# An attention and MoE kernel whose written order of steps is made anew, with seven more warm-up products

## The chip, the cores and the metric

The kernel runs on 1 core of one Trainium2 chip. The metric is the device time of one execution in microseconds (us), the median of several runs. PE (TensorE) multiplies matrices into PSUM, which is made of eight banks; DVE (VectorE) and ACT (ScalarE) read PSUM and write the on-chip memory; POOL (GpSimd) works on the on-chip memory alone; SP (SyncE) issues most of the transfers.

## The reference

```python
def _attn_ref(x, state):          # x 8x8x512x64, state 8x8x32x64
    scores = scale * np.matmul(x, state.transpose(0, 1, 3, 2))
    ...
    xread = np.matmul(a, state)              # a = softmax(scores)
    scores2 = scale * np.matmul(state, x.transpose(0, 1, 3, 2))
    ...
    sread = np.matmul(a2, x)                 # a2 = softmax(scores2)
    return np.concatenate([xread, sread], axis=2)

def _moe_ref(x, g_ln, w_ch1, w_ch2):         # x 8x544x512 from the attention
    xn = (x - mu) / np.sqrt(var + 1e-06) * g_ln
    ch = np.maximum(xn @ w_ch1, 0.0) @ w_ch2
    return x + ch
```

For each of 8 batches there are two small softmax attentions between x (512 rows, 8 heads) and state (32 rows). Their results, 544 rows of 512 numbers, go through a layer norm and a two-layer perceptron of 512, 2048 and 512 numbers, and are added to it. Everything is float32; the kernel keeps that precision by splitting each number into two float16 halves (hi and lo) and adding three products.

## The kernel before, in words

**Units.** The hidden layer's 2048 numbers are taken in four parts, u = 0 to 3. For each batch, a matrix for each part (`state_products`, tile `matrix`) folds state and the first weights together, so the first layer is a product of `matrix` with the attention's numerators `ea`. Batch 0 goes by simple loops while the weights are still being read and split. Batches 1 to 7 go by `products(b)`: two halves g of the rows, four parts u, so 56 units. Four more units (`products(B)`, first stage on L839) do the 32 state rows of all batches.

**One unit.** PE makes two banks `half` on L829, 12 products each (`block(1)`, then `block(0)`). Every one is read by both ACT and DVE. Of `block(1)`, ACT copies a part into `rs` and a part into `xs` (the hi half), and DVE makes a difference in `rs` and the lo half in `xs`. Of `block(0)`, ACT copies hi into `xs`, and DVE makes three sums in `rs` and the lo half. Then ACT and POOL turn the sums in `rs` into hi and lo halves in `xs` (`strassen_hidden`). With these, PE makes 42 products on L887 into four banks `acc`, by Strassen's scheme (`strassen_products`, four steps of 18, 6, 12 and 6 products, with the weights `w2h` and their prepared sums `sums`). After four units `together` adds the banks up in `strip` and `xr` and stores them. The pool of `half` has two banks and the pool of `banks` one pair, so PE can fill one again only when all its readers are done.

**Attention.** While the units of one batch run, the attention of the next is made between them: load of x in two pieces (`x_f`) and of state, split (`x16`) and transposing transfers, scores (L430) in `banks`, the softmax steps on DVE, ACT and POOL (`ts`, `mA`, `mB`, `dA`, `eB`, `eb`, `ef`, `ea`, most of them 128 x 1024 elements), a read of the state (L507). Then eight transfers copy `ea` to `ek`, one copies the upper part of `ek` from the lower, and the product on L537 (`mix`) reads `ek`.

**What sets the order.** All steps are recorded as streams of closures. `issue` calls them in the order that the table `PLAN` gives: an item `67:62` is step 62 of stream 67. Each engine runs its instructions in that order; between engines the program waits by semaphores, which the recording layer places from the order and from what each step reads and writes. It also orders any two reads of one PSUM bank by two engines: the one that is written later waits for the other. The products of `warmth`, `WARM` of them, multiply ones into a bank that nobody reads; the plan puts them where PE has nothing to do in the first 40 us.

```python
def issue(tc, streams, plan):
    streams = [list(s) for s in streams]
    with tc.manual_schedule():
        for item in plan.split() or [f"{k}:0-{len(s)}" for k, s in enumerate(streams)]:
            k, n = item.split(":")
            n = [int(v) for v in n.split("-")]
            for f in streams[int(k)][n[0]:n[-1] + 1]:
                f()
```

Of the kernel before, what the change touches and what calls it, by code (L numbers as in the profile page):

```python
# [165 lines left out]
)  # L166
WARM = 112


class Later:  # L170
# [832 lines left out]
```

## Time and profile before

| | |
|---|---|
| median of 3 runs | 682.26 us (679.79 to 683.41) |
| the profiled execution, its own time | 682.87 us |
| its span, first to last instruction | 680.8 us |
| mean granted clock of PE | 0.995 |
| read from HBM, written | 28.05 MB, 9.44 MB |
| busy share: PE, DVE, ACT, POOL | 94%, 73%, 54%, 33% |

The page gives for each engine the time in which it worked and, in forty slices of the span, how much of each was work. A row of the waits says which engine and line stood, which engine and tile it waited for, and how long in total, how often and at most. A row of the timeline gives start, length, engine, line, operation, tile written and tiles read, sizes and count, and in brackets how long the engine stood idle before it and who ended that. Matmuls are pipelined: two rows that follow each other overlap in the records. Most steps are recorded on L192, the helper `do`, so they are told apart by their tiles.

### The profile page before, as it was taken

How to read it: one execution, taken by the hardware profiler on the slowest of the kernel's cores; microseconds unless marked ns; L12 is line 12 of the kernel's file. 1: busy time of each engine (PE TensorE's matmuls, PEld its weight loads, DVE VectorE, ACT ScalarE, POOL GpSimd, SP SyncE). 2: the span in 40 equal slices, each digit the busy share in tenths (PEclk: the TensorE clock that was granted, in tenths of full speed). 3: DMA queues.
4: the chain of work that ended last, by engine and by line, in shares of the span. 5: the costliest groups of instructions: out<-in, count | busy, mean ns of one | idle time of the engine just before them, and what ended most of it. 6: DMA issues, size and time to landing. Idle time of an engine off the chain costs nothing. (4 is left out here: it accounts for less than half of the span.)

```text
span 680.8 us, 15966 instructions
## 1 busy us (share of the span) xinstructions
PE 643.0 (94%) x6640; PEld 501.3 (74%) x6640; DVE 495.1 (73%) x990; ACT 367.0 (54%) x659; POOL 225.1 (33%) x189
## 2 busy tenths in 40 slices
PE   9999999999999998999999999988999999999995
PEld 3455655768778786778777878776878777888885
DVE  3999996767668688677867796678568786665443
ACT  4589976755454654475546554655276434353341
POOL 0015224411335324413623363145323451333231
PEclk9999999999999999999999999999999999999999
DMA  8976766330032533404250416052311225011002
GB/s 312 279 258 253 204 115 141 64 111 5 19 59 55 150 68 101 112 34 87 55 140 32 104 27 161 23 99 65 82 37 30 43 40 151 32 34 24 9 1 93
DMA packets 90039, 63.15 MB, mean 93 GB/s; under 512 B 69296, under 2 KB 82096, under 8 KB 89520
## 3 DMA queue, kind: packets, MB, share of 16 engines
q1 hardware_dynamic: 87696, 58.18, 32.4%
q0 software_dynamic: 864, 3.15, 2.4%
q8 instruction: 52, 0.85, 0.5%
q10 hardware_dynamic: 1408, 0.82, 0.4%
q14 instruction: 19, 0.16, 0.1%
HBM read 28.05 MB, written 9.44 MB: 55 GB/s over the span
## 5 line engine op out<-in xcount | busy, mean ns | idle before, releaser
L887 PEld LDWEIGHTS <-xs 128*128 128x128 f16 x2520 | 243.7, 98 | 40.8 <-issue 7.9
L192 POOL TENSOR_TENSOR xs<-rs,xs 128x512 f16<-128x512 f32 x120 | 143.3, 1202 | 282.8 <-ACT xs L192 196.4
L887 PE MATMUL acc<-w2h,xs 128*128 128x256 f16 x1440 | 182.7, 274 | 0.0
L829 PE MATMUL half<-ea,matrix 128*128 128x256 f16 x1344 | 163.1, 274 | 14.1 <-DVE rs L192 5.9
L829 PEld LDWEIGHTS <-matrix 128*128 128x128 f16 x1344 | 128.8, 98 | 39.2 <-DVE xs L192 8.4
L887 PE MATMUL acc<-sums,xs 128*128 128x256 f16 x1080 | 143.7, 273 | 2.9 <-DVE strip L192 1.6
L192 DVE SCALAR_TENSOR_TENSOR rs<-half,rs 128x256 f32<-128x256 f32 x224 | 90.6, 417 | 48.9 <-ACT rs L192 21.2
L192 ACT ACTIVATE xs<-rs 128x512 f16<-128x512 f32 (+1 forms) x128 | 77.6, 618 | 67.6 <-DVE rs L192 61.2
L192 ACT ACTIVATE xs<-half 128x256 f16<-128x256 f32 (+1 forms) x112 | 54.1, 486 | 71.5 <-DVE rs L192 41.8
L192 DVE SCALAR_TENSOR_TENSOR xs<-half,xs 128x256 f16<-128x256 f32 (+1 forms) x112 | 60.9, 548 | 24.9 <-ACT xs L192 22.0
L192 ACT ACTIVATE rs<-half 128x256 f32<-128x256 f32 x56 | 21.2, 379 | 48.5 <-PE half L829 37.9
L192 DVE SCALAR_TENSOR_TENSOR matrix<-banks,hs,matrix 128x1024 f16<-128x1024 f32 x28 | 35.8, 1279 | 15.6 <-ACT matrix L192 15.6
L745 PE MATMUL acc<-w2h,hid 128*128 128x512 f16 x192 | 43.4, 379 | 0.3 <-POOL hid L192 0.3
L192 DVE TENSOR_TENSOR strip<-acc,strip 128x256 f32<-128x256 f32 (+1 forms) x60 | 32.9, 548 | 10.6 <-PE acc L887 6.5
L192 ACT ACTIVATE matrix<-banks,hs 128x1024 f16<-128x1024 f32 x28 | 31.1, 1111 | 15.3 <-PE banks L690 14.4
L745 PEld LDWEIGHTS <-hid 128*128 128x128 f16 x192 | 18.2, 98 | 21.4 <-POOL hid L192 0.8
L192 POOL TENSOR_TENSOR hid<-strip,hid 128x512 f16<-128x512 f32 x16 | 20.4, 1285 | 27.9 <-ACT hid L192 25.8
L192 POOL TENSOR_TENSOR ts<-ts,mA 128x1024 f32<-128x1024 f32 (+1 forms) x8 | 16.2, 2022 | 39.3 <-DVE of_weights L192 28.3
L192 PE MATMUL half<-ones 128*128 128x512 bf16 x112 | 27.8, 401 | 1.1 <-DVE ones L322 1.1
L192 DVE SCALAR_TENSOR_TENSOR xr<-strip,of_second,xr 128x512 f32<-128x512 f32 x28 | 26.1, 933 | 2.8 <-POOL strip L192 2.7
L192 ACT ACTIVATE x<-x_f,x_s 128x512 f16<-128x512 f32 x32 | 21.7, 715 | 11.0 <-DVE x_s L192 11.0
L192 DVE SCALAR_TENSOR_TENSOR x<-x_f,x_s,x 128x512 f16<-128x512 f32 x32 | 24.9, 799 | 3.7 <-ACT x L192 3.2
(149 smaller groups left out, 785.0 us busy)
## 6 DMA issues: line engine op xcount, KB each, us to landing
raw<-in_moe_w_ch_dram SPq DMA_DIRECT2D x10, 1024.0 KB, 8.4
out_dram<-xr SPq DMA_DIRECT2D x16, 512.0 KB, 3.3
x_f<-in_x_dram SPq DMA_DIRECT2D x15, 512.0 KB, 5.1
sums<-in_moe_w_ch_dram SPq DMA_DIRECT2D x6, 1024.0 KB, 7.6
ek<-ea SPq DMA_DIRECT2D x56, 64.0 KB, 2.0
ek<-ek SPq DMA_DIRECT2D x7, 512.0 KB, 4.3
xr<-part POOLq DMA_DIRECT2D x6, 512.0 KB, 4.9
s_r<-in_state_dram SPq DMA_DIRECT2D x28, 64.0 KB, 3.5
```

Source lines behind the costliest of these rows:

```text
L192: return lambda: f(*map(now, args), **{k: now(v) for k, v in kw.items()})
L745: nc.tensor.matmul(po, lhsT=hid[:, i, q, c * P:(c + 1) * P], rhs=w[:, j, q], start=first and q == 0 and n == 0, stop=last and q == 3 and n ...
L829: nc.tensor.matmul(ps[:, 256 * q:256 * q + 256], lhsT=m[:, h, i, P * (2 * k + q):P * (2 * k + q) + P], rhs=ea[:, 0, j, h, 256 * g:256 * g ...
L887: nc.tensor.matmul(po[o], lhsT=y[:, n, i, o] if o < 2 else x[:, o - 2, n, i], rhs=v[j], start=u == 0 and n == 0 and k == 0 and o in (2, 1, ...
```

## The change

`PLAN` is written anew as a whole, and `WARM` goes from 112 to 119. Nothing else differs: the same 2554 steps of the streams beside the warm-up, with the same sizes, buffers and operations, are called in another order. One line of the table on each side:

```diff
-    "176:12 176:8 176:11 176:10 176:13-16 "
+    "176:1-2 176:4-5 175:3 176:3 157:9 176:6-7 166:8 176:9-11 176:8 176:12 176:15 176:14 176:16 176:13 "
...
-WARM = 112
+WARM = 119
```

One line shorter, every line number behind the table is less by one: L829 before is L828 after, and L192 is L191.

Two places. The first is DVE in the softmax of batch 6, while units of batch 5 run. `half_6618` and `half_6702` before, `half_6584` and `half_6641` after, are the two banks of one unit; mA, mB, dA and eb are softmax steps. Before:

```order
L192 SCALAR_TENSOR_TENSOR rs_6647<-half_6618,rs_6647 128x256
L192 TENSOR_SCALAR mB_6644<-mB_6644,es_6398 128x2
L192 TENSOR_REDUCE dA_6693<-ts_6632 128x32
L192 SCALAR_TENSOR_TENSOR xs_6690<-half_6618,xs_6690 128x2x128
L192 TENSOR_SCALAR dA_6693<-dA_6693 128x32
L192 TENSOR_SCALAR rs_6716<-mv_6251 128x4
L192 RECIPROCAL dA_6693<-dA_6693 128x32
L192 SCALAR_TENSOR_TENSOR eb_6700<-eB_6697,eb_6700 128x1024
L192 SCALAR_TENSOR_TENSOR rs_6647<-half_6702,rs_6647 128x256
L192 SCALAR_TENSOR_TENSOR xs_6690<-half_6702,xs_6690 128x2x256
L192 SCALAR_TENSOR_TENSOR rs_6647<-half_6702,rs_6647 128x256 x2
```

And after, on the same engine for the same unit:

```order
L191 SCALAR_TENSOR_TENSOR rs_6658<-half_6584,rs_6658 128x256
L191 STREAM_TRANSPOSE ts_6686<-banks_6620 128x1024
L191 TENSOR_REDUCE mA_6688<-ts_6686 128x32
L191 SCALAR_TENSOR_TENSOR rs_6658<-half_6641,rs_6658 128x256
L191 TENSOR_REDUCE mB_6706<-banks_6620 128x2
L191 SCALAR_TENSOR_TENSOR rs_6658<-half_6641,rs_6658 128x256
L191 SCALAR_TENSOR_TENSOR xs_6690<-half_6641,xs_6690 128x2x256
L191 TENSOR_SCALAR mB_6706<-mB_6706,es_6654 128x2
L191 SCALAR_TENSOR_TENSOR xs_6690<-half_6584,xs_6690 128x2x128
L191 TENSOR_REDUCE dA_6744<-ts_6686 128x32
L191 TENSOR_SCALAR dA_6744<-dA_6744 128x32
L191 SCALAR_TENSOR_TENSOR rs_6658<-half_6641,rs_6658 128x256
```

The first read of the second bank moved from behind dA and eb to ahead of mB and dA; eb now comes behind all reads of both banks.

The second place is SP around the copies of `ek` for batch 3. Before:

```order
L192 DMA ek_3841<-ea_3754 32x2x512 x8
L192 DMA sread_rows_104<-sread_3864 32x128
L192 DMA s_r_3982<-in_state_dram 32x8x64
L192 DMA sread_rows_104<-sread_3864 32x128
L192 DMA ek_3841<-ek_3841 64x4096
L192 DMA s_r_3982<-in_state_dram 32x8x64 x3
```

And after:

```order
L191 DMA ek_3758<-ea_3737 32x2x512 x8
L191 DMA ek_3758<-ek_3758 64x4096
L191 DMA sread_rows_104<-sread_3961 32x128
L191 DMA x_f_4013<-in_x_dram 128x4x256
L191 DMA sread_rows_104<-sread_3961 32x128
```

The large copy now follows the eight small ones directly; behind it stand a small store and then a 512 KB load of x_f, where three loads of state stood.

243 rows, old and new, of the table PLAN are left out of this document.

## The prediction

> **What bounds the kernel now.** I read the page first, then what PE waited for, then the timeline around the longest of those waits.
>
> ```profile
> span 680.8 us, 15966 instructions
> PE 643.0 (94%) x6640; PEld 501.3 (74%) x6640; DVE 495.1 (73%) x990; ACT 367.0 (54%) x659; POOL 225.1 (33%) x189
> ...
> PE   9999999999999998999999999988999999999995
> ...
> DVE  3999996767668688677867796678568786665443
> ...
> PEclk9999999999999999999999999999999999999999
> ```
>
> PE is busy in every slice, at the full granted clock, and no other engine comes near it. The work is the same before and after, so only three things can change: the time in which PE stands, the warm-up products that fill its first 40 us, and the tail behind its last product.
>
> ```profile
> 672.22 1.47 PE L887 MATMUL acc<-w2h,xs 128*128 128x256 f16 x12
> ...
> 675.90 1.74 SPq L192 DMA_DIRECT2D out_dram<-xs  x4
> ```
>
> PE ends at 672.22 + 1.47 = 673.7 us and was busy for 643.0, so it stood for **30.7 us**. The tail is 680.8 - 673.7 = 7.1 us. This is what PE stood for (us in total, times, longest):
>
> ```profile
> PE half L829 <- DVE rs L192: 5.9, 4, 2.8
> PE half L829 <- DVE xs L192: 5.6, 7, 1.7
> PE banks L537 <- DMA ek<-ek: 4.5, 3, 2.0
> PE half L829 <- DVE of_second L192: 1.6, 1, 1.6
> PE acc L887 <- DVE strip L192: 1.6, 2, 1.1
> PE banks L690 <- DVE matrix L192: 1.2, 1, 1.2
> PE half L192 <- DVE ones L322: 1.1, 1, 1.1
> ...
> PE acc L639 <- DVE raw L192: 1.0, 1, 1.0
> PE banks L537 <- PE acc L777: 1.0, 1, 1.0
> ...
> PE half L829 <- ACT xs L192: 0.7, 2, 0.4
> ...
> PE acc L639 <- DVE sums L192: 0.5, 1, 0.5
> ```
>
> Rows on `half` at L829 are PE waiting for a bank whose old content ACT and DVE haven't yet read: 5.9 + 5.6 + 1.6 + 0.7 = **13.8 us**. Rows on L537 are the product that needs the loaded tile ek: 4.5, and 1.0 for batch 1, which I count with it (the row names PE, but that product needs ek too): **5.5 us**. The other 30.7 - 13.8 - 5.5 = 11.4 us are scattered, 2.6 of them in the first 40 us (the rows of ones, raw and sums).
>
> **Reads of one bank.** One of the longest waits, and the largest one:
>
> ```profile
> 548.35 0.60 ACT L192 ACTIVATE xs<-half 128x512 f16<-128x512 f32 x1 [4.97 <-DVE rs L192]
> 549.03 1.16 PE L829 MATMUL half<-ea,matrix 128*128 128x256 f16 x9 [1.67 <-DVE xs L192]
> ...
> 470.76 2.56 DVE L192 SCALAR_TENSOR_TENSOR eb<-eB,eb 128x1024 f16<-128x1024 f32 x1 [0.58 <-ACT eb L192]
> 473.24 0.41 DVE L192 SCALAR_TENSOR_TENSOR rs<-half,rs 128x256 f32<-128x256 f32 x1
> 473.69 0.60 ACT L192 ACTIVATE xs<-half 128x512 f16<-128x512 f32 x1 [2.47 <-DVE rs L192]
> 474.92 0.75 DVE L192 SCALAR_TENSOR_TENSOR rs<-half,rs 128x256 f32<-128x256 f32 x2
> 475.73 1.59 PE L829 MATMUL half<-ea,matrix 128*128 128x256 f16 x9 [2.83 <-DVE rs L192]
> ```
>
> ACT's copy of `half` into xs uses nothing that DVE's rs makes, yet it stood for 4.97 and 2.47 us until that rs had been read out of the same bank: the program makes the second reader of a bank wait for the first, in the written order. DVE's rs was late itself, queued behind the wide eb, and PE waited at the end of it for 1.67 and 2.83 us.
>
> The new order moves this. In each of the 56 units two banks are read by both engines, 112 in all. Counted in the two orders (each sequence of readers by engine, leaving out changes of engine where the second needs the first's data), the reader changes engine 116 times before and 94 times now; ACT follows DVE with no other step written between 15 times before and 2 times now. At the 2.83 us place the first DVE read of the second bank now stands ahead of mB and of dA, and far ahead of eb. So the change does what it says there.
>
> How much of 13.8 us goes? If it went with all changes of engine, 94 of 116 would be left and the saving is 13.8 x 22/116 = 2.6; if with the closest ones, 2 of 15 are left and it is 12.0. Below nothing it can go too (the last rival). The 2.47 us wait is of the close kind and the 4.97 us one is DVE's own queue, so I take the middle, **-6.9**.
>
> At that place there is a second cause. The same eb took 1.37 us at another place, and 2.56 here, with a POOL operation beside it:
>
> ```profile
> 472.19 2.00 POOL L192 TENSOR_TENSOR rs<-rs,mhalf 128x4 f32<-128x4 f32 x1
> ...
> 543.77 1.37 DVE L192 SCALAR_TENSOR_TENSOR eb<-eB,eb 128x1024 f16<-128x1024 f32 x1
> ```
>
> That is 1.2 of the 2.83 us which no order of bank reads removes. The Trainium skill, SBUF — State Buffer, "Who interferes with whom", speaks against the change here: a DVE instruction with two SBUF inputs shares a read interface with GpSimd, and one of them blocks. By that page the loss lies in DVE and POOL meeting, and the bank term would shrink towards nothing; the 2.56 against 1.37 us agrees with it at this one place.
>
> **Loads.**
>
> ```profile
> ek<-ek SPq DMA_DIRECT2D x7, 512.0 KB, 4.3
> ...
> 283.93 0.52 SPq L192 DMA_DIRECT2D ek<-ek  x1
> ...
> 289.95 0.91 PE L537 MATMUL banks<-sk,ek 128*128 128x64 f16 x16 [1.95 <-DMA ek<-ek]
> ...
> 497.76 0.77 PE banks L690 x24
> ...
> 526.13 1.31 PE half L829 x12
> 527.44 1.97 PE acc L887 x18
> ```
>
> ek is copied in two steps, eight small transfers and then the large one, 4.3 us in the median and here 289.95 - 283.93 = 6.0. What hides it is the PE work written between the step that makes ea's second half (DVE) and the product. By the last three rows, 1.31 / 12 = 0.109 us a product, this cover was 9.6 us for batch 3 and is 13.3 now, and 8.1 and now 12.1 for batch 4; for batch 2 it falls from 16.0 to 13.9. On SP the large copy now follows the small ones directly, where two small stores and a load stood between; what follows it is a 512 KB load of x_f, no longer three small ones, which may slow it. The added cover of 3.7 and 4.0 us is over the longest wait, 2.0. The saving lies between 0 (the loads in flight grow by as much) and 5.5; I take **-4.5**, leaving one wait of 1.0 for batch 2.
>
> The Trainium skill, DMA: Bandwidth & Descriptors, "Anatomy of one DMA", gives about 2.0 us and 436 KB a us for a DMA, which makes an estimate of 3.2 us for 512 KB; by that the cover was enough already and nothing is gained. The 4.3 and 6.0 us here disagree, and the measured waits decide.
>
> **Warm-up.**
>
> ```profile
> 11.71 5.35 PE L192 MATMUL half<-ones 128*128 128x512 bf16 x24
> ...
> 39.12 3.07 PE L639 MATMUL acc<-raw,gm 128*128 128x512 f32 x6 [1.01 <-DVE raw L192]
> ...
> 20.00:40.00 20.00, 18.07 (x146) 8.55 (x145) 18.62 (x35) 12.80 (x15) 1.05 (x1) 1.00 0.78 254
> 80.00:100.00 20.00, 19.85 (x144) 10.23 (x142) 19.62 (x39) 14.96 (x19) 5.18 (x5) 1.00 0.66 140
> ```
>
> Seven products of 5.35 / 24 = 0.22 us are added: 1.5 us on PE. They lie in front of products that waited for DVE (0.5 and 1.0 us in the waits above), in a stretch where DVE (third pair in the windows) is busy for 18.6 and later 19.6 of 20 us. If DVE sets the time they cost 0, if PE does, 1.5. I take **+0.7**.
>
> **The rest.** The last 42 products, the DVE steps after them and the stores stand in the same order; the tail stays at 7.1. The products of the last unit start 5.9 us of PE work behind the last first-stage product, where 9.2 lay before; the steps between (on ACT and DVE one copy of 0.6, three reads of 0.4, another copy of 0.6 and a subtraction of 0.7) make some 3.2, so it stays covered. The other 11.4 us of waits are places that the new order moves as well, and nothing says where to: 0, with -4 to +4 as its bounds, a third of them each way.
>
> **Sum:** -6.9 - 4.5 + 0.7 = -10.7 us. The profiled execution took 682.87 us, 2.1 around its span of 680.8, and lies 0.6 above the median, 682.26. From the median: 682.3 - 10.7 = 671.6, so **672**.
>
> **Rivals.**
> - **Loads alone.** The waits on `half` are DVE's queue and its meetings with POOL, not reads of banks (for it: 4.97 us in a queue and 2.56 us for eb; against: the close crossings fall from 15 to 2). 682.3 - 4.5 + 0.7 = 678.5. Chance 0.17, two thirds of it within 0.5%.
> - **More goes.** All of 13.8 and 5.5 and 4 of the rest: 682.3 - 13.8 - 5.5 - 4 + 0.7 = 659.7. For it: nearly all the closest crossings go, and the loads' cover grows by more than their waits. Against: at 24 places (32 before) ACT still follows DVE with no PE work written between. Chance 0.13 for 666 or less.
> - **Nothing changes**, the order differs and the waits move: 682. Chance 0.04.
> - **Slower: wide steps between reads of one bank.** Between the first and the last DVE read of a bank there stands at least one DVE step of 1.1 us or more at 30 banks (27 before), and two or more at 13 (7 before). Each holds the bank from PE, as eb did. It decides where they and the reads last longer than the PE work until the bank's next use, which is 4 us or less at 16 banks now, 15 before. Six more such places at 1.9 us (the mean of the four longest waits on `half`: 2.83, 1.67, the 1.6 of its third row, and 1.42 below) are 11.4: 682.3 - 4.5 + 0.7 + 11.4 = 690. Against it: 85 banks free of wide steps before and 82 now is nearly the same. Chance 0.14.
>
> ```profile
> 204.30 0.94 PE L829 MATMUL half<-ea,matrix 128*128 128x256 f16 x7 [1.42 <-DVE rs L192]
> ```
>
>
> **How the numbers follow.** The forecast (667 to 677) has 0.52. The range of 662 to 685 leaves out half of "more goes" and most of "slower". A difference under 0.5% (3.4 us) is what a measurement here can't tell from no change. Faster: 0.52 + 0.13 + a third of 0.17 = 0.71; the same: 0.11 + 0.04 = 0.15; slower 0.14.
>
> **What would show it.** In the changed profile, PE busy is about 644.5 and its idle time before its last product some 18 to 20 us; the L537 row on ek is under 1.5; the rows of `half` on DVE and ACT together are 5 to 9, and the 2.83 us wait in the softmax of the last batch but one is gone. If the `half` rows stay near 13 with long DVE steps before them, "loads alone" or "slower" was right; if the L639 and L690 waits vanish and the product of L507 still comes 1.5 us later, the warm-up was paid in full.

## The result, and the profile after

| | before | after |
|---|---|---|
| median, us | 681.31 (679.79 to 683.41, 4 runs) | 662.80 (662.01 to 663.94, 4 runs) |
| the profiled execution | 682.87 | 663.94 |
| its span | 680.8 | 662.1 |

The ratio is 0.9728, with a 95% interval of 0.9694 to 0.9761: 18.5 us less, where the forecast had 10.7 less. The page of the changed kernel, its first lines, and from its timeline PE's last products and the last stores:

```profile
span 662.1 us, 15974 instructions
PE 641.5 (97%) x6647; PEld 502.0 (76%) x6647; DVE 496.2 (75%) x990; ACT 368.3 (56%) x659; POOL 220.6 (33%) x189
...
653.89 1.47 PE L886 MATMUL acc<-w2h,xs 128*128 128x256 f16 x12
...
657.57 1.74 SPq L191 DMA_DIRECT2D out_dram<-xs  x4
```

PE ends at 653.89 + 1.47 = 655.4 and stood for 13.9 us before that, where it was 30.7. The tail is 6.7 us (7.1). DVE does the same work in about the same time (496.2 us, 495.1 before). What PE waited for now, the rows that the text uses:

```profile
PE half L828 <- DVE xs L191: 2.5, 3, 1.2
...
PE half L828 <- DVE rs L191: 1.0, 3, 0.5
PE banks L536 <- issue: 1.0, 1, 1.0
...
PE half L828 <- DVE matrix L191: 0.7, 2, 0.4
```

The rows on `half` at L828 are 2.5 + 1.0 + 0.7 = 4.2 us (13.8 before). The row on L536 is 1.0 (5.5); it names no releaser, but it lies in batch 4, whose large copy took 6.3 us and landed 0.1 us before the product began. All others together 13.9 - 4.2 - 1.0 = 8.7 (11.4). So of the 18.6 us of span, waits on `half` gave 9.6, loads 4.5, other waits 2.7. The warm-up products cost 1.6 more, by their groups in the two profiles:

```profile
L192 PE MATMUL half<-ones 128*128 128x512 bf16 x112 | 27.8, 401 | 1.1 <-DVE ones L322 1.1
```

```profile
L191 PE MATMUL half<-ones 128*128 128x512 bf16 x119 | 29.4, 399 | 1.1 <-DVE ones L321 1.1
```

PE's other products show 643.0 - 27.8 = 615.2 us before and 641.5 - 29.4 = 612.1 now, 3.1 less for the same instructions; the tail gave 0.3. An estimate covers most of the 3.1: a product's record is 0.273 us long and adds 0.109 where the next one overlaps it, so each gap between PE's records costs 0.164 us of busy time; there are 50 gaps before and 35 now, which makes 15 x 0.164 = 2.5. The sum is -9.6 - 4.5 - 2.7 + 1.6 - 3.1 - 0.3 = -18.6.

The place of the prediction's 2.83 us wait, in the timeline of the changed kernel:

```profile
461.02 2.08 DVE L191 SCALAR_TENSOR_TENSOR eb<-eB,eb 128x1024 f16<-128x1024 f32 x1
...
461.98 2.00 POOL L191 TENSOR_TENSOR rs<-rs,mhalf 128x4 f32<-128x4 f32 x1
...
465.35 0.83 PE L886 MATMUL acc<-w2h,xs 128*128 128x256 f16 x6 [0.37 <-DVE xs L191]
```

eb is slow here too, 2.08 us with a POOL step beside it. But PE has 38 products of L886 to work on from 460.66 to 464.97 us, and stands for only 0.37 us behind them.

**Five stretches.** One table explains more than the waits do. Each row below is the stretch from the scores of a batch (L430, L429 after) to the product that reads ek (L537, L536), for batches 2 to 6 (batch 1 overlaps the front, and batch 7's L537 comes 59 us behind its scores): the stretch in us from the span's start, its length, PE's busy time in it. Before:

```profile
195.20:227.80 32.60, 29.41 (x358) 1.00 0.27 59
256.30:290.00 33.70, 28.35 (x329) 1.00 0.41 97
323.10:351.90 28.80, 26.47 (x300) 1.00 0.36 78
390.90:420.10 29.20, 27.80 (x310) 1.00 0.30 63
460.60:493.30 32.70, 29.87 (x317) 0.95 0.32 71
sum 157.00, PE 141.89; mean PE 28.38
```

And after:

```profile
196.10:224.30 28.20, 27.73 (x348) 1.00 0.33 74
249.60:280.50 30.90, 29.32 (x340) 1.00 0.27 58
318.40:349.30 30.90, 29.20 (x340) 1.00 0.36 88
386.40:420.30 33.90, 33.41 (x394) 1.00 0.43 97
449.80:479.80 30.00, 29.18 (x341) 1.00 0.42 104
sum 153.90, PE 148.84; mean PE 29.77
```

The five stretches together are about as long as before, 153.9 and 157.0 us, and PE stands in them for 5.1 us in place of 15.1. That is 10.0 of the 16.8 us of idle time that went. PE's work in them grew by 7.0 us, but the sums hide where. In batches 2, 3 and 6 PE stood for 3.2, 5.4 and 2.8 us, and now for 0.5, 1.6 and 0.8: 8.5 of the 10.0. Its work there is no larger (87.6 us before, 86.2 now); these three stretches got shorter, from 99.0 to 89.1 us. The added work lies in batches 4 and 5 (54.3 and 62.6 us), where PE had stood for only 3.7 us. (In batch 6 before, PE's granted clock was 0.95, and its work there is somewhat inflated by that.) Before, the product that ends a stretch begins within 0.2 us of the landing of ek in all five, so the chain sets their length; now it begins 0.1 to 1.4 us behind it.

DVE's second step on ea, from which the transfers to ek follow, shows where the stretches got shorter. Batch 2 before, and after:

```profile
196.27 1.22 DVE L192 TENSOR_REDUCE mB<-banks 128x2 f32<-128x1024 f32 x1 [1.56 <-PE banks L430]
...
200.53 1.25 DVE L192 STREAM_TRANSPOSE ts<-banks 128x1024 f32<-128x1024 f32 x1 [2.19 <-ACT eB L192]
...
215.13 1.21 DVE L192 SCALAR_TENSOR_TENSOR ea<-ef,ea 128x1024 f16<-128x1024 f32 x1
```

```profile
197.16 1.25 DVE L191 STREAM_TRANSPOSE ts<-banks 128x1024 f32<-128x1024 f32 x1
...
201.49 1.22 DVE L191 TENSOR_REDUCE mB<-banks 128x2 f32<-128x1024 f32 x1
...
211.81 1.22 DVE L191 SCALAR_TENSOR_TENSOR ea<-ef,ea 128x1024 f16<-128x1024 f32 x1
```

ts begins the way to ea (ts, mA, dA, ef, ea). Before, it was written behind mB and eB, and DVE stood for 2.19 us until ACT's eB had read the same scores; now it comes first. Counted from the start of its stretch, the ea step begins at 19.9, 19.1, 16.8, 17.2 and 18.7 us before, and at 15.7, 17.9, 16.4, 19.1 and 16.5 now. It comes sooner in batches 2, 3 and 6, by 7.7 us of the 9.9, and later only in batch 5, where mB is now written ahead of ts and the stretch is the longest. No run changes this order alone, so it is read from the traces and not shown by an experiment.

### The profile page after: what moved, and what is told of

It is laid out like the page before. It is cut to its first block, busy times and chain, and to the rows that moved or that the text cites. A ratio compares the mean times of both kernels' runs of the same rounds, so it can differ in the third digit from the quotient of the medians.

```text
span 662.1 us, 15974 instructions
## 1 busy us (share of the span) xinstructions
PE 641.5 (97%) x6647; PEld 502.0 (76%) x6647; DVE 496.2 (75%) x990; ACT 368.3 (56%) x659; POOL 220.6 (33%) x189
## 5 line engine op out<-in xcount | busy, mean ns | idle before, releaser
L886 PEld LDWEIGHTS <-xs 128*128 128x128 f16 x2520 | 243.5, 98 | 41.3 <-issue 9.8
L191 POOL TENSOR_TENSOR xs<-rs,xs 128x512 f16<-128x512 f32 x120 | 142.0, 1195 | 291.5 <-ACT xs L191 189.5
L886 PE MATMUL acc<-w2h,xs 128*128 128x256 f16 x1440 | 182.2, 273 | 2.1 <-POOL xs L191 0.8
L828 PE MATMUL half<-ea,matrix 128*128 128x256 f16 x1344 | 162.5, 273 | 4.6 <-DVE xs L191 2.5
L828 PEld LDWEIGHTS <-matrix 128*128 128x128 f16 x1344 | 128.9, 98 | 27.1 <-issue 6.3
L886 PE MATMUL acc<-sums,xs 128*128 128x256 f16 x1080 | 142.6, 273 | 0.7 <-DVE strip L191 0.7
L191 DVE SCALAR_TENSOR_TENSOR rs<-half,rs 128x256 f32<-128x256 f32 x224 | 90.0, 418 | 36.2 <-ACT rs L191 15.7
L191 ACT ACTIVATE xs<-rs 128x512 f16<-128x512 f32 (+1 forms) x128 | 77.2, 620 | 69.6 <-DVE rs L191 58.7
L191 ACT ACTIVATE xs<-half 128x256 f16<-128x256 f32 (+1 forms) x112 | 53.4, 487 | 85.5 <-PE half L828 31.8
L191 DVE SCALAR_TENSOR_TENSOR xs<-half,xs 128x256 f16<-128x256 f32 (+1 forms) x112 | 61.2, 549 | 21.0 <-ACT xs L191 20.7
L744 PE MATMUL acc<-w2h,hid 128*128 128x512 f16 x192 | 44.8, 390 | 0.1
L191 DVE SCALAR_TENSOR_TENSOR matrix<-banks,hs,matrix 128x1024 f16<-128x1024 f32 x28 | 35.8, 1278 | 10.5 <-ACT matrix L191 10.3
L191 DVE TENSOR_TENSOR strip<-acc,strip 128x256 f32<-128x256 f32 (+1 forms) x60 | 33.1, 552 | 9.3 <-PE acc L886 7.0
L191 ACT ACTIVATE rs<-half 128x256 f32<-128x256 f32 x56 | 21.4, 381 | 32.2 <-PE half L828 27.3
L744 PEld LDWEIGHTS <-hid 128*128 128x128 f16 x192 | 18.7, 100 | 23.1 <-issue 3.0
L191 ACT ACTIVATE matrix<-banks,hs 128x1024 f16<-128x1024 f32 x28 | 31.1, 1110 | 5.7 <-PE banks L689 5.5
L191 POOL TENSOR_TENSOR hid<-strip,hid 128x512 f16<-128x512 f32 x16 | 22.4, 1415 | 25.2 <-ACT hid L191 23.6
L191 PE MATMUL half<-ones 128*128 128x512 bf16 x119 | 29.4, 399 | 1.1 <-DVE ones L321 1.1
L191 POOL TENSOR_TENSOR ts<-ts,mA 128x1024 f32<-128x1024 f32 (+1 forms) x8 | 14.7, 1842 | 40.2 <-DVE of_weights L191 28.9
L191 DVE SCALAR_TENSOR_TENSOR x<-x_f,x_s,x 128x512 f16<-128x512 f32 x32 | 26.9, 863 | 1.1 <-ACT x L191 1.0
L191 DVE BATCH_NORM_STATS2 s<-xr 128x6 f32<-128x512 f32 x32 | 21.8, 683 | 6.9 <-ACT xr L191 6.9
L191 DVE SCALAR_TENSOR_TENSOR xr<-strip,of_second,xr 128x512 f32<-128x512 f32 x28 | 24.6, 889 | 0.3
```

Source lines behind the costliest of these rows:

```text
L191: return lambda: f(*map(now, args), **{k: now(v) for k, v in kw.items()})
L744: nc.tensor.matmul(po, lhsT=hid[:, i, q, c * P:(c + 1) * P], rhs=w[:, j, q], start=first and q == 0 and n == 0, stop=last and q == 3 and n ...
L828: nc.tensor.matmul(ps[:, 256 * q:256 * q + 256], lhsT=m[:, h, i, P * (2 * k + q):P * (2 * k + q) + P], rhs=ea[:, 0, j, h, 256 * g:256 * g ...
L886: nc.tensor.matmul(po[o], lhsT=y[:, n, i, o] if o < 2 else x[:, o - 2, n, i], rhs=v[j], start=u == 0 and n == 0 and k == 0 and o in (2, 1, ...
```

## The experiments

Three theories. **Changes of engine** (the prediction's): PE waits because the second reader of a bank waits for the first, and the new order has fewer and wider-spaced changes. **DVE's queue**: the reads stand behind wide DVE steps. **The chain**: the softmax between scores and L537 takes its time whatever is done about one bank, so the stall goes only if the chain itself gets shorter or more PE work is put beside the whole of it.

In the diffs a unit's steps are 0 and 5 (PE fills its two banks), 1 and 2 (ACT reads the first), 3 and 4 (DVE reads the first), 6 (ACT reads the second), 7 to 10 (DVE reads the second). Streams 67 and 127 are the attention of batches 3 and 6.

**1. Fewer changes of engine in the order of before.** 62 ACT reads go ahead of DVE's reads of the same bank; the first of them:

```diff
-    "29:3 29:7 25:21 29:2 29:4 "
+    "29:2 29:3 29:7 25:21 29:4 "
```

> The order of before with one kind of step moved: in each bank of half, ACT's reads are written ahead of DVE's wherever the data allow it (62 of 75 ACT reads that stood behind a DVE read; with no other step between, ACT follows DVE once instead of 15 times). Theory 'bank order' (ACT, held behind DVE's read of the same bank, is what delays PE): the waits on half fall from 13.8 us to about 5 and the time by 5 to 10 us. Theory 'DVE's queue' (DVE's reads come late because of wide steps ahead of them, whoever reads first): the waits on half stay within 2 us of 13.8 and the time within 2 us of before.

Measured: 684.17 us beside 680.83, ratio 1.0046 (1.0021 to 1.0071), though ACT stands directly behind DVE once and not 15 times, and the reader changes engine 100 times and not 116, counted as in the prediction. PE's rows on `half` are 9.4 + 3.2 + 1.6 = 14.2 us (13.8 before), the two larger:

```profile
PE half L829 <- DVE xs L192: 9.4, 8, 2.1
...
PE half L829 <- DVE rs L192: 3.2, 4, 1.9
```

Two rows of before, from the waits of all engines:

```profile
ACT xs L192 <- DVE rs L192: 102.9, 75, 5.0
...
DVE rs L192 <- ACT xs L192: 14.5, 17, 2.3
```

And the same two here:

```profile
ACT xs L192 <- DVE rs L192: 78.5, 65, 4.2
...
DVE rs L192 <- ACT xs L192: 50.7, 33, 4.9
```

By these rows ACT waits 24.4 us less, DVE 36.2 more: the wait is handed to the other engine. Changes of engine alone are not what PE paid for.

**2. Wide DVE steps out of the way.** In the order of before, 20 wide softmax steps go behind the last DVE read of a bank. One of them, mB of batch 3:

```diff
-    "67:39 56:3 58:2 60:0 58:4 67:40 "
+    "56:3 58:2 60:0 58:4 67:39 67:40 "
```

> The order of before with 20 wide DVE steps of the attention (ts, mA, mB, dA, eb, ef, ea) moved from between the first and the last DVE read of a bank of half to behind the last. Theory 'DVE's queue': the waits on half fall by 4 to 8 us of 13.8, and the time by 3 to 7 us unless the softmax now comes late. Theory 'bank order': the waits on half fall by at most 2 us, since ACT still stands behind DVE as often.

Measured: 695.84, ratio 1.0209 (1.0162 to 1.0255). PE's waits here:

```profile
PE acc L888 <- DVE strip L193: 7.9, 3, 3.1
PE half L830 <- DVE rs L193: 6.0, 3, 3.9
PE half L830 <- DVE xs L193: 6.0, 5, 3.9
```

The rows on `half` are as large as before, and strip comes 7.9 us late. The edit moves a wide step behind one bank and so ahead of the next. The five stretches, taken as in the table above, get longer too, 168.1 us in sum (157.0 before), with 148.5 us of PE's work in them (141.9). Waits are not all of the loss, though. Of the 15.7 us of span (696.5 and 680.8), 5.6 are PE's idle time (36.3 and 30.7), and 10.1 are its busy time:

```profile
PE 653.1 (94%) x6640; PEld 506.5 (73%) x6640; DVE 500.5 (72%) x990; ACT 367.9 (53%) x659; POOL 225.4 (32%) x189
```

The mean granted clock of PE is 0.978 (0.995): it was halved seven times, for 24.9 us of PE's work, where it was halved once before, for 3.4.

**3. No large copy.** In this kernel the product on L537 uses only the lower 64 rows, which leaves the low halves of the state out of it, so the copy inside ek isn't needed.

```diff
-            yield do(nc.sync.dma_start, out=ek[64:128], in_=ek[0:64])
+            yield lambda: None
...
-                                         lhsT=ek[:, h % 2, h // 2, (2 * t + c) * P:(2 * t + c + 1) * P],
-                                         rhs=sk[:, h], start=True, stop=True, skip_group_check=True)
+                                         lhsT=ek[0:64, h % 2, h // 2, (2 * t + c) * P:(2 * t + c + 1) * P],
+                                         rhs=sk[0:64, h], start=True, stop=True, skip_group_check=True)
```

> The order of before without the 512 KB copy within ek; the product on L537 then uses the lower 64 rows of ek and sk alone, so the low halves of the state are left out of it. Theory 'loads': the 5.5 us of waits on L537 go to under 1 and the time falls by 4 to 6 us. Theory that these waits are hidden by later ones (PE would wait at the next bank anyway): the waits on L537 go, those on half grow by as much, the time falls by under 2 us.

Measured: 676.11 beside 680.83, ratio 0.9932 (0.9899 to 0.9966), which is 4.7 us (2.3 to 6.9). Rows on `half` (6.0, 5.6 and 1.6) are unchanged. The loads are a term of their own, of about the forecast size. The edit also takes seven transfers of 512 KB out of the queue and halves the rows of these products; what that alone gives was not separated.

**4 and 5. ACT reads late, in the changed order.** In both, 35 ACT reads of `half` go to a later place: in the first right behind a DVE read of their bank, in the second just ahead of that same DVE read. The first of the 35, 29:2, in the two:

```diff
-    "29:0 29:1 29:2 27:7 ... 29:3 29:7 "
+    "29:0 29:1 27:7 ... 29:3 29:2 29:7 "
```

```diff
-    "29:0 29:1 29:2 27:7 ... 29:3 29:7 "
+    "29:0 29:1 27:7 ... 29:2 29:3 29:7 "
```

> The changed order with the bank reads made worse: 35 ACT reads of half are moved to right behind a DVE read of the same bank (37 such neighbours, 2 in the changed kernel, 15 before). Theory 'bank order': the waits on half grow from 4 us to 8 to 14 and the time by 4 to 10 us against the changed kernel's 662.8. Theory 'DVE's queue': within 2 us of 662.8.

> The changed order again, as a control to the run that put 35 ACT reads of `half` right behind a DVE read of the same bank (671.0 us). Here the same 35 ACT reads go to the same places in the written order but stand just ahead of that DVE read. If what costs time is that ACT must wait for a DVE read that stands late in its queue, most of the 8.2 us go away here: 662.8 to 666. If what costs time is only that the ACT reads are written late (their banks are held longer, whoever reads last), this is as slow as that run: 669 to 672. If DVE now waits for ACT in turn, as when ACT was put first in the order of before, something between: 666 to 669, with more waits of DVE's rs and xs on ACT xs.

Measured: 670.99, ratio to before 0.9843 (0.9814 to 0.9871), and 669.30, ratio 0.9845 (0.9820 to 0.9870): 8.2 and 6.5 us of the gain are lost by the medians, 7.8 and 8.0 by the ratios, and the two are alike, though ACT stands directly behind DVE 37 times in one and 4 times in the other. The groups of first-stage products (total, mean, idle before them), in this order:

```profile
L830 PE MATMUL half<-ea,matrix 128*128 128x256 f16 x1344 | 162.6, 273 | 7.8 <-DVE xs L193 4.7 <-DVE rs L193 2.5 <-DVE matrix L193 0.3
```

```profile
L830 PE MATMUL half<-ea,matrix 128*128 128x256 f16 x1344 | 162.5, 273 | 7.5 <-DVE xs L193 5.6 <-DVE rs L193 1.4 <-DVE matrix L193 0.3
```

By these two, where an ACT read stands matters; whether it follows DVE's read or DVE's read follows it doesn't. That is the second place at which the prediction's mechanism falls. One doubt is left: in the second run DVE's rs waits for ACT's xs for 20.4 us (7.4 in the changed kernel), so a part of its loss can be the same wait the other way round. The chain theory doesn't cover this loss either: PE stands for 19.2 and 19.6 us before its last product (13.9 in the changed kernel), but in the five stretches, taken as in the table above, for only 6.8 and 5.6 (5.1).

**6. The reads ahead at the eight longest waits.** What does DVE do while PE waits? In the profiled run of before, the timeline has 15 waits of 0.1 us or more at L829, 14.0 us together. From the end of the products that filled such a bank to the end of its last read is 89.3 us for the 15. DVE's rows in them add up to 23.4 us of reads of the bank and 61.4 of other steps, but rows that follow each other overlap. With each moment counted once, DVE read the bank for 22.3, did only other steps for 53.9, and stood for 13.1. (The expectation below goes by the sums of rows, which leave 4.5.) So in this experiment the reads go ahead of those other steps (eb, mA, ef, ts, rf, x) at eight banks. One of the eight edits is the diff of the next experiment.

> The order of before, with the reads of `half` moved ahead of DVE's steps of another kind (eb, mA, ef, ts, rf, the split of x) at the eight banks that PE waited for longest (1.62, 1.42, 1.01, 0.80, 1.21, 2.83, 0.98 and 1.67 us, 11.5 in sum), nothing else. Changes of engine stay at 116, close ones of ACT behind DVE go from 15 to 17. In the trace of before DVE worked on other steps for 61.4 of the 89.3 us in which the waited-for banks were held, and stood for only 4.5. If that queue is what PE waited for, most of the 11.5 us go, less what the delayed softmax steps then cost: 671 to 677 beside 681, with `half` rows of 3 to 8. If changes of engine cost the time, as the forecast had it, nothing goes: 680 to 683. If the delayed steps come late instead, as when all wide steps were moved, slower than 683, with new waits on strip, ea or matrix.

Measured: 684.98 beside 679.08, ratio 1.0092 (1.0057 to 1.0126). PE's waits:

```profile
PE half L831 <- DVE xs L194: 9.3, 11, 1.8
PE acc L889 <- POOL xs L194: 2.8, 2, 1.5
PE acc L889 <- ACT xs L194: 2.4, 1, 2.4
...
PE banks L509 <- DMA ebT<-eb: 2.2, 1, 2.2
```

The rows on `half` come down from 13.8 to 10.8 (these 9.3, and 0.8 and 0.7 further down), and xs and eb are late instead. PE's idle time before its last product is 30.5 us, as before (30.7).

**7 and 8. One place, one move and two.** The place of the 2.83 us wait. First the reads alone (127:44 is eb):

```diff
-    "127:54 127:44 118:7 118:6 127:55 118:10 118:8 120:0 118:9 "
+    "127:54 118:7 118:6 118:10 118:8 118:9 127:44 127:55 120:0 "
```

> The order of before with one place edited, that of the 2.83 us wait in the softmax of batch 6: the five reads of the second bank of `half` (DVE rs, xs, rs, rs and ACT xs) go ahead of DVE's eb. In the run with eight places edited this wait went and PE stood for 2.15 us a little later, at L507, for the transposed copy of eb. If that is a handover from one wait to the other, the 2.83 us row goes here too, a wait of L507 on ebT of 1.8 to 2.3 us comes, and the time falls by under 1 us: 678 to 682. If the reads alone were the cause, 2.8 us less and no new wait.

Then the same, and the product that needs eb (127:56) 2.6 us of PE work later, with the one after it (127:58):

```diff
-    "119:0 127:60 127:47 127:56 ... 121:0 117:0 "
+    "119:0 127:60 127:47 ... 121:0 127:56 117:0 "
```

> The same edit, and the product of L507 that needs eb (with the step that reads it and the product after that) written 2.6 us of PE work later, behind two steps of L887. If PE's wait is handed on because both the reads and this product lie within the time of one DVE queue, both waits are gone now, and PE's idle time before its last product is 28 us in place of 30.7: 2 to 3 us less time than before. If the next consumer (matrix, strip or ek) is late in turn, a new wait of 1 us or more stands there, and nothing is gained.

Measured: 679.67 beside 680.72, ratio 0.9982 (0.9964 to 1.0000), and 680.31, ratio 1.0007 (0.9989 to 1.0025). The first in the timeline, where the 2.83 us wait is gone, and a second wait stands 2 us on:

```profile
475.30 1.64 PE L509 MATMUL banks<-ebT,x 128*64 128x64 f16 x64 [2.17 <-DMA ebT<-eb]
```

The second, with eb earlier than any wait of PE's and the stall 5 us later, at the unit's products:

```profile
471.14 1.02 POOL L194 TENSOR_TENSOR rs<-rs,mhalf 128x4 f32<-128x4 f32 x1
...
471.95 1.21 DVE L194 SCALAR_TENSOR_TENSOR eb<-eB,eb 128x1024 f16<-128x1024 f32 x1
...
478.46 0.61 PE L889 MATMUL acc<-w2h,xs 128*128 128x256 f16 x4 [1.40 <-DVE xs L194]
```

and its waits on ek, of which the longest is that of batch 6, which did not wait before:

```profile
PE banks L539 <- DMA ek<-ek: 4.9, 3, 2.5
```

2.83 us became 2.17, and then 1.40 + 2.50. Batch 6's stretch from its scores to L537, in the first and in the second:

```profile
457.10:489.20 32.10, 29.67 (x316) 0.95 0.36 86
```

```profile
459.50:492.40 32.90, 28.65 (x316) 1.00 0.31 71
```

It was 32.7 us before, with 29.87 of PE work. Whichever wait is taken away, PE comes to its next product earlier and waits there, and the stretch stays at 32.1 to 32.9 us. This is what the chain theory says, at this one place. PE's clock differs between the two (0.95 and 1.00 in the rows), so some of the 1.0 us by which PE's work is less in the second, and of the wait that it adds, is the clock's.

**9. The same edit in the changed order,** at the four longest waits that are left there; one of them:

```diff
-    "138:2 147:39 147:40 147:41 127:75 138:6 138:4 138:3 "
+    "138:2 138:4 138:3 147:39 147:40 147:41 127:75 138:6 "
```

> The changed order, with the same edit at the four banks that PE still waited for longest (1.16, 0.91, 0.50 and 0.43 us, 3.0 in sum). If DVE's queue is the cause there too: 660 to 662 beside 662.8, with `half` rows near 1.5 in place of 4.2. If the steps moved back come late: 663 to 666, with new waits on xs, strip or ea.

Measured: 661.56 (661.25 to 663.36), ratio to before 0.9735 (0.9710 to 0.9760), the same as the changed kernel within the interval. PE's idle time is 13.6 us (13.9), the rows on `half` 2.0 (4.2), and two new rows, on sT (1.1) and on ek (0.9), make it up.

So no version here is shown to beat the changed kernel.

**10 and 11. The front and the warm-up.** First the changed order up to the first step of batch 1's units (29:0) and the order of before behind it; then the changed order without its last seven warm-up products:

```diff
-WARM = 119
+WARM = 112
```

> The changed order up to the first step of batch 1's units, with its 119 warm-up products, and the order of before from there on. If the gain comes from the units (reads of banks, loads), this is as before: 680 to 683 beside 681.3. If the front and its warm-up carry part of it, less than 679; if the seven products are paid in full with nothing in return, 682 to 683.

> The changed order with the last seven of its warm-up products left out, so 112 as before. The forecast's term was +0.7 for them: 662.1 here beside 662.8. If they stood on the path of the first 40 us, 661.3; if DVE sets that stretch's time, 662.8, with 1.5 us more idle time of PE; if the products keep the clock up, slower than 662.8.

Measured: 686.09 beside 679.62, ratio 1.0088 (1.0061 to 1.0116), so the front alone gains nothing (the seam of the two orders may cost some of the 6.5 us). And 663.62, ratio to before 0.9765 (0.9739 to 0.9790): not distinguishable from the changed kernel, whose span is 662.1 where this has 662.0. PE's busy time from 40 to 60 us is, in the changed kernel and here:

```profile
40.00:60.00 20.00, 18.88 (x268) 0.99 0.83 288
```

```profile
40.00:60.00 20.00, 17.42 (x260) 0.97 0.83 283
```

The seven products, 1.5 us, fill time in which PE stands otherwise. No cost of theirs shows; without them the time is if anything longer, by 0.8 us of the medians. The mean granted clock is 0.996 in both.

**12. Half and half.** The changed order up to batch 5's units, the order of before from there.

> The changed order up to the first step of batch 5's units, the order of before from there on. If the gain is spread over the batches (reads of banks in every unit, loads in batches 2 to 7), about half of 18.5 us is here: 670 to 673. If it sits in a few places of the first half, 663 to 666; of the second half, 678 to 681. The 2.83 us wait of the softmax of batch 6 should stand here again, since it lies in the part that is as before.

Measured: 673.62, ratio 0.9908 (0.9882 to 0.9933). One row of its waits on `half`:

```profile
PE half L830 <- DVE rs L193: 3.2, 2, 2.8
```

The 2.8 us wait is back with its part of the order. The time lies just outside the 670 to 673 that a gain spread evenly would give: the first four batches, in the new order, bring 0.9 of the 2.7% that the whole order brings (the seam may cost some). In the profile, 9.2 of the 16.8 us of idle time are gone (21.5 us of it are left, 13.9 in the changed kernel). So the gain is spread over the batches, and how much of it lies ahead of batch 5's units stays rough: a third by the times, over half by the idle time.

## Why the prediction was right, and where it wasn't

The forecast was 672 with a range of 662 to 685, and 662.80 came: inside the range by 0.8 us, outside the band of 667 to 677 that had a chance of 0.52. The direction follows from the argument; that the number fell inside the range is in part luck, since the largest term rested on a wrong cause.

**The bound and the three places of the gain: right.** PE sets the time. Idle time fell by 16.8 us, on `half`, at L537 and in the rest; PE's busy time and the tail stayed within 2 us.

**Reads of one bank: right in direction, the size too small and the cause wrong.** The step that failed is the one that scaled 13.8 us by changes of engine, between 2.6 and 12.0, and took 6.9. It measured 9.6. Fewer changes gained nothing (1), and delaying ACT's reads in the changed order cost much the same with 37 close changes as with 4 (4, 5). The sentence that held is the aside that DVE's rs "was late itself, queued behind the wide eb": in 53.9 of 89.3 us DVE does only other steps (6). But taking the reads ahead of that queue doesn't help either (2, 6, 7). A stall at one bank is where PE runs into a chain that ends at L537, and in the new order this chain is 9.9 us shorter in the three batches in which PE stood longest. That it is shorter is measured; that this is why most of the idle time in the stretches went, 8.5 of 10.0 us, is argued from them, and from 7 and 8, which were made at one place. Which moved steps shorten it was not tested alone. Outside the five stretches idle time fell by another 6.8 us, where reads that stand early enough must matter (4, 5). No part of the order was found that gives the 9.6 us by itself.

**Loads: right in size, the reason in part.** 4.5 forecast and 4.5 in the rows; the copy's whole worth is 4.7 (3). The median to landing is no shorter than before, 4.4 us and 4.3:

```profile
ek<-ek SPq DMA_DIRECT2D x7, 512.0 KB, 4.4
```

But the cover, taken as PE's work between the end of DVE's ea step and the product, grew as forecast in batch 4 alone (8.9 us and 11.9). In batch 2 it is 10.4 and 10.8, in batch 3 11.4 and 10.7. Batch 3 had the longest wait, and what went there is time of the copy itself: 5.9 us in the one execution, 4.1 in the other. And the 5.5 us were one execution, near the top: all rows on this product in the profiles of orders of before that keep the copy come to 4.2 us (1), 3.3 (2), 2.1 (6), 1.6 (7), 5.7 (8) and 1.8 (10). That 4.5 met 4.5 is in part luck. As to the estimate of 3.2 us, the Trainium skill, DMA: Bandwidth & Descriptors, "Anatomy of one DMA", gives its figures for transfers that GpSimd issues in software; these copies are SP's.

**Warm-up: +0.7 forecast, no cost seen** (11). "If DVE sets the time they cost 0" was the right end. PE's group of them is 1.6 us larger, and its waits that much shorter.

**The rest: 0 forecast, -2.7, inside the bounds of 4 each way.** Not in the sum at all were 3.1 us by which PE's other products show less busy time; by the estimate above, 2.5 of them come with the waits that went. The prediction took PE to be "at the full granted clock"; it was halved for 3.4 us right behind the 2.83 us wait, and in the changed kernel for as long in the front.

**Rivals.** "More goes", 659.7, came nearest: it had all 13.8, 5.5 and 4 of the rest, and 9.6, 4.5 and 2.7 went. "Loads alone" (678.5) falls by the `half` rows. "Slower" falls: banks with a wide DVE step between their reads are 30 as counted, and the rows on `half` fell; taking such steps out made the kernel slower (2). The signs were: PE busy 644.5 (641.5 came), idle 18 to 20 (13.9), L537 under 1.5 (1.0), `half` 5 to 9 (4.2), the 2.83 us wait gone (gone).

**The rule against the change.** The Trainium skill, SBUF — State Buffer, "Who interferes with whom", has a DVE step with two SBUF inputs contend with a GpSimd step that reads SBUF, so that one of them blocks. The rows agree about the step: eb took 2.56 us and 2.08 with a POOL step beside it, and 1.21 when that step ended 0.2 us after eb began (8). What the prediction drew from it for the bank term did not come: the meeting is still there after the change, but PE has other products and stands for 0.37 us in place of 2.83.

## What to carry to other kernels

A wait at one buffer inside a long dependent chain is no price by itself: measure the chain from its first product to its last, and how much work of the bounding engine is written beside it, and do so chain by chain, since a sum over five of them hid where the gain was. Making one link earlier handed the wait to the next, in the one place where it was tried. A shorter chain took time away (the copy left out, 4.7 us). And look at a second execution before a transfer's wait is put into a sum.

## What the runs showed of the hardware

The order of before takes 677.46 to 683.48 us over the 23 runs of its largest set, the changed one 662.01 to 663.94 over 4. The rows on L537 of before show a part of such scatter: 5.5 us in its own profile, 1.6 in that of experiment 7 (0.6 + 0.6 + 0.4), whose copies for batches 2 to 5 are as in before. The copies' median of 4.3 us is the same in both, but that of batch 3 took 5.9 us in the one and 4.4 in the other. In the changed kernel five of the seven took 4.1 to 4.4 us, and two 5.9 and 6.3. That an order which covers them is also steadier is not shown; 4 runs are few to see it by.

PE's granted clock falls to half now and then, for 3.4 us at a time (once for 6.8). In before it does so once ahead of the tail, 0.6 us behind the end of the 2.83 us wait; PE's row of the windows there:

```profile
476.00:480.00 4.00, 4.00 (x24) 0.57 0.36 70
```

The 24 products take 0.167 us each, where the prediction found 0.109 elsewhere. In the changed kernel it falls once too, at 59.6 us; in experiments 4 and 9 not at all ahead of the tail, and in 2 seven times. If it is the wait that sets this off, a wait costs more than its row says; what sets it off was not tested.
